# Swapped activations of block 1: shifted DMA transposes of the normalised tiles in place of copies between partition halves

## The chip, the cores and the metric

The kernel runs on one core of one Trainium2 chip. The metric is the device time of one execution in microseconds (us); the runs shown are three, with their median. Engines are named as the profile names them: PE (matrix unit, TensorE), PEld (its weight loads), DVE (VectorE), ACT (ScalarE), POOL (GpSimd), SP (SyncE, which here only issues DMAs).

## What is computed

One sequence of 2048 rows with 448 features goes through a layer norm without weights. The normalised rows feed two branches, and both are added to the input:

```python
x = A_x                                   # [1, 2048, 448] bf16
xn = _layernorm(x)
# A: 16 heads of 28, causal attention over a window of 256 keys
q, k, v = split_heads(xn @ A_wqkv)
p = softmax(where(0 <= i - j < 256, q @ k.T * 28 ** -0.5, -1e9))
a = merge_heads(p @ v) @ A_wo
# B: gated feed-forward, 448 -> 1792 -> 448
b = (gelu(xn @ B_w_gate) * (xn @ B_w_up)) @ B_w_down
return x + a + b
```

## The kernel before

**Tiling.** The 2048 rows are 16 tiles of 128 rows (`NT`), and four blocks of 512 columns once transposed (`NB`, `QB`). The 448 features are three and a half groups of 128, or seven chunks of 64. PE needs the activations with features on the partitions, so each normalised tile `xn` is transposed into `xnT`, `[128, 4, 2048]`: groups 0 to 2 hold features 0 to 383 (chunk c on the lower 64 partitions for even c, on the upper 64 for odd c), group 3 holds chunk 6, features 384 to 447, on both halves.

**Paired half matmuls.** Seven chunks of 64 rows fill half of PE's rows. The kernel therefore runs two products side by side, one on the lower half of the rows (`hi` 0), one on the upper (`hi` 1): two tiles of v (`v_pair`, L325), q and k of one group of heads (`qk_pair`, L339), two column groups of the gate or up matrix (`chunk`, L494). Each goes through all seven chunks, so each half needs every chunk on its own partitions. Chunks with `c % 2 == hi` lie there in `xnT`, chunk 6 lies on both; the others come from a copy with the halves exchanged, `xsw` `[128, 3, 1024]`. `xchunk` (L486) picks the source. `xsw` is a ring of two blocks (`ring`, L246): blocks 0 and 2 in its first 512 columns, 1 and 3 in the second.

**How the transposes and swaps are made.** Block 0's four tiles are transposed on PE (`transp`, L186). Tiles 4 to 15 are transposed by DMA from SP's queue (`dma_transp`, L182). For them `norm` (L165) writes 512 columns: the 448 features and, in columns 448 to 511, features 384 to 447 again, so that group 3 comes out with chunk 6 on both halves. `swap` (L473) then issues two DMAs from SBUF to SBUF, one for each half. Block 0 is swapped at once (L775), blocks 2 and 3 at the head of blocks 1 and 2 (L876), block 1 in two parts of two tiles each inside `ahead3`.

**Order around the change.** The order of work on each engine is written out by hand. Block 0's attention runs eight steps; the list `plan` says what is put between them. After the first steps come `ahead` (loads `wvs`, v's weights with halves exchanged), `ahead2` (statistics, `norm` and transpose of tile 4) and `ahead3` (L814): the same for tiles 5 to 7, the first part of block 1's swap, `fill_pads` on POOL, `swap_weights` (two DMAs that fill `wsq`, the exchanged weights of q and k), the second part of the swap, and the loads of `wg`, `wu`, `x_sb`, `wo` and `wd`. All those DMAs stand in SP's queue in this order, and a DMA whose input is not ready holds the queue. The first work on block 1 is `gen_pairs(1, ...)` (L847), from step 6 of block 0: v of tiles 4 and 5, v of tiles 6 and 7, then q and k of groups 0 to 2. Then block 0's gated part begins, with `wg`.

`w3p` holds the weights of q and k for chunk 6; `q_last` (L257) multiplies all 128 partitions of group 3 of `xnT` with it for heads 12 to 15, where its upper half is zero. `general_path` (L939) is a fallback behind a branch at the end, for inputs whose softmax sums leave the range; it is not taken here.

Of the kernel before, what the change touches and what calls it, by code (L numbers as in the profile page):

```python
# [16 lines left out]
S, D, H, Dh, F = 2048, 448, 16, 28, 1792  # L17
P = 128
NT = S // P
NF = F // P  # L20
QB, NB = 512, 4
# [6 lines left out]
def kernel(  # L28
# [11 lines left out]
    nc = tc.nc  # L40
# [31 lines left out]
    def rows(w, c0, n):  # L72
        return w[c0 * P:(c0 + n) * P, :].rearrange("(c p) n -> p c n", p=P)

    def load_ffn(dst, w, pairs):

        wv64 = w.rearrange("(c p) (h n) -> p c h n", p=64, h=2)
        ns = slice(pairs.start * P, pairs.stop * P)  # L80
        for hi in range(2):
            nc.sync.dma_start(out=dst[64 * hi:64 * hi + 64, :, ns], in_=wv64[:, :, hi, ns])
# [54 lines left out]
    xnT = const.tile([P, 4, S], bf16, name="xnT")  # L137
    xsw = const.tile([P, 3, 2 * QB], bf16, name="xsw")
# [24 lines left out]
    xns = {}  # L163

    def norm(t):  # L165
        xn = work.tile([P, 4, P], bf16, name="xn", bufs=4)
        xf = xn[:, :, :].rearrange("p a b -> p (a b)")
        both = ((0, D, 0), (D, 64, 384))
        for lo, n, src in both if t > 3 else both[:1]:
            nc.vector.tensor_scalar(out=xf[:, lo:lo + n], in0=x_sb[:, t, src:src + n], scalar1=mv_all[:, t, 0:1],  # L170
                                    scalar2=rstd_all[:, t:t + 1], op0=ALU.subtract, op1=ALU.mult)
        xns[t] = xn
# [8 lines left out]

    def dma_transp(t):  # L182

        nc.sync.dma_start_transpose(out=xnT[:, :, t * P:(t + 1) * P], in_=xns.pop(t)[:, :, :].rearrange("p a b -> p (a b)"))

    def transp(t, copy, tag):  # L186

# [58 lines left out]
    def ring(qb):  # L246

        return slice(qb % 2 * QB, (qb % 2 + 1) * QB)
# [39 lines left out]
    def fill_pads(last):  # L288


        def put(dst, src, n, lo):

            src = src.rearrange("p (j d) -> p j d", d=Dh)[:, :, lo:]
            if n == 4:
                nc.gpsimd.tensor_copy(out=dst[:, 12:16, Dh:32], in_=src[:, :, 24:28])
            src = src[:, :, 0:24].rearrange("p j (g i) -> p g j i", i=8)[:, :, :, 0:4]
            nc.gpsimd.tensor_copy(out=dst[:, 0:12, Dh:32].rearrange("p (g j) i -> p g j i", j=4), in_=src)

        if not last:
            for c in range(3):  # L300
                k = wraw[:, c, D + 12 * Dh:2 * D]
                put(wqp[:, c, :, :], k, 4, 0)
                put(wkp[:, c, :, :], k, 3, 4)
            return
        put(w3p[0:64, :, :], w3k[0:64, :], 4, 0)
        put(w3p[64:128, :, :], w3k[64:128, :], 3, 4)
        nc.gpsimd.memset(w3p[64:128, 12:16, :], 0.0)
# [165 lines left out]
    def swap(qb, t=None, n=4):  # L473

        t0 = P * (4 * qb if t is None else t)
        to = t0 - qb * QB + ring(qb).start
        for hi in range(2):
            nc.sync.dma_start(out=xsw[64 * hi:64 * hi + 64, :, to:to + n * P],
                              in_=xnT[64 - 64 * hi:P - 64 * hi, 0:3, t0:t0 + n * P])

    def swap_weights():

        for hi, src in enumerate((wqp, wkp)):
            nc.sync.dma_start(out=wsq[64 * hi:64 * hi + 64], in_=src[64 - 64 * hi:P - 64 * hi, 0:3])

    def xchunk(qb, hi, c, t0, n):  # L486

        r = slice(64 * hi, 64 * hi + 64)
        if c == 6 or c % 2 == hi:
            return xnT[r, c // 2, t0:t0 + n]  # L490
        t0 += ring(qb).start - qb * QB
        return xsw[r, c // 2, t0:t0 + n]

    def chunk(pair, w, p, qb, c):  # L494

# [318 lines left out]
    def ahead3():  # L814
        for t in (5, 6, 7):
            norm(t)
            dma_transp(t)
        swap(1, 4, 2)
        fill_pads(False)
        swap_weights()  # L820
        swap(1, 6, 2)
        load_ffn(wg, B_w_gate, slice(0, 3))
        load_ffn(wg, B_w_gate, slice(3, 7))
        load_ffn(wu, B_w_up, slice(5, 7))
        nc.sync.dma_start(out=x_sb[:, 12:16, :], in_=xv[:, 12:16, :])
        wo_v = A_wo.rearrange("(g j d) n -> j d g n", g=4, j=4)
        tail = A_wo[14 * Dh:, :].rearrange("(t i) n -> i t n", i=4)
        for j, (t0, n) in enumerate(SLOTS):
            nc.sync.dma_start(out=wo[32 * j:32 * j + Dh, 0:n, :], in_=wo_v[j][:, 0:n])
            nc.sync.dma_start(out=wo[32 * j + Dh:32 * j + 32, 0:n, :], in_=tail[:, t0:t0 + n])  # L830
        for k in range(0, NF, 7):
            nc.sync.dma_start(out=wd[:, k:k + 7, :], in_=rows(B_w_down, k, 7))
# [106 lines left out]
def general_path(tc, locals_):  # L939

    nc = tc.nc
    L = locals_
    x_sb, xnT, qT, kT, v_sb, wd, wo, ident = (L[k] for k in ("x_sb", "xnT", "qT", "kT", "v_sb", "wd", "wo", "ident"))
    with ExitStack() as st:
# [11 lines left out]
        swap = keep.tile([P, P], bf16, name="gswap")  # L956
        for hi in range(2):
            nc.vector.tensor_copy(out=swap[:, 64 * hi:64 * hi + 64], in_=ident[:, 64 - 64 * hi:P - 64 * hi])
        for qb in range(NB):
            ts = slice(qb * QB, (qb + 1) * QB)  # L960
            for c in range(3):
                pg = ps.tile([P, QB], f32, name="pg", tag="pg")
                nc.tensor.matmul(pg[:, :], lhsT=swap[:, :], rhs=xnT[:, c, ts], start=True, stop=True)
                nc.vector.tensor_copy(out=L["xsw"][:, c, 0:QB], in_=pg[:, :])
            for f in range(NF):
                hi, p = divmod(f, 7)
                r = slice(64 * hi, 64 * hi + 64)
                pg = ps.tile([P, QB], f32, name="pg", tag="pg")
                pu = ps.tile([P, QB], f32, name="pu", tag="pu")
                for dst, w in ((pg, L["wg"]), (pu, L["wu"])):  # L970
                    for c in range(7):
                        x = xnT[r, 3, ts] if c == 6 else xnT[r, c // 2, ts] if c % 2 == hi else L["xsw"][r, c // 2, 0:QB]
                        nc.tensor.matmul(dst[:, :], lhsT=w[r, c, p * P:(p + 1) * P], rhs=x, start=(c == 0), stop=(c == 6),
                                         tile_position=(64 * hi, 0))
                ge = wk.tile([P, QB], bf16, name="gge")
                nc.scalar.activation(out=ge[:, :], in_=pg[:, :], func=ACT.Gelu_apprx_tanh)
                nc.vector.tensor_tensor(out=hT[:, f, :], in0=ge[:, :], in1=pu[:, :], op=ALU.mult)
            for g in range(4):
                pg = ps.tile([P, QB], f32, name="pg", tag="pg")
                for c in range(4):  # L980
                    n, w = (64, L["w3p"]) if c == 3 else (P, L["wqp"][:, c, :, :])
# [3 lines left out]
            for tt in range(4):  # L985
# [6 lines left out]
                for h in range(H):  # L992
                    g, r = h // 4, slice(32 * (h % 4), 32 * (h % 4) + Dh)
# [23 lines left out]
                for j, (t0, n) in enumerate(SLOTS):  # L1017
                    c = 4 * (t0 % 7)
                    nc.vector.tensor_copy(out=o_sb[:, j:j + 4 * n - 3:4, Dh:32],
                                          in_=o_sb[:, 14 + t0 // 7, c:c + 4 * n].rearrange("p (g i) -> p g i", i=4))  # L1020
# [43 lines left out]
```

## Time and profile before

| | us |
|---|---|
| runs shown | 211.73, 211.86, 212.12; median 211.86 |
| profiled execution, its time | 212.1 |
| its span, first to last instruction | 210.3 |
| granted PE clock over the span | 1.000 |

The span is what the profile's rows are measured in, from 0 at the first instruction; the profiled execution's own time is 1.8 us longer. In the profile's groups and timelines a row names engine, source line, operation, the tile written, `<-`, the tiles read, and the shape; `x4` is a count of instructions merged into the row. Square brackets give the idle time of the engine before the row and what ended it. In SP's rows the duration is that of issuing the DMA, not of the transfer.

### The profile page before, as it was taken

The page shows a single profiled execution, that of the slowest core. Times are in us where ns is not written, and L with a number is a line of the kernel's source. Part 1 is how long each engine was busy: PE and PEld are TensorE (multiplying, and loading weights), DVE is VectorE, ACT ScalarE, POOL GpSimd, SP SyncE. Part 2 cuts the span into 40 slices and gives each one's busy share as a digit, 9 for nine tenths or more (in the row PEclk, how much of TensorE's full clock was granted, in tenths as well). Part 3 has the DMA queues.
Part 4 walks back from the last instruction along what each step waited for, and adds up shares of the span by engine and source line. Part 5 has one row for each costly group of instructions (what it writes and reads, how often), then busy time and mean ns, then how long its engine had stood idle before and what let it go on. Part 6 is the DMA issues. An engine that isn't in the chain of part 4 may idle for free. (4 is left out here: it accounts for less than half of the span.)

```text
span 210.3 us, 6672 instructions
## 1 busy us (share of the span) xinstructions
PE 205.5 (98%) x2842; PEld 98.8 (47%) x2842; DVE 156.3 (74%) x359; ACT 134.6 (64%) x132; POOL 43.8 (21%) x87
## 2 busy tenths in 40 slices
PE   7999999999999999999999999999999999999994
PEld 2444444544454445444445444544444454544572
DVE  6898899899788985696438897395385699596532
ACT  4799896956677977413778788523587787756000
POOL 5389902260000220040000112013000022032000
PEclk9999999999999999999999999999999999999999
DMA  6999989959431001003421000100000010100011
GB/s 171 254 238 230 94 199 223 248 147 254 101 88 42 25 15 28 9 4 67 75 75 47 24 4 24 23 3 20 23 5 0 3 47 3 48 5 16 3 47 50
DMA packets 24890, 15.68 MB, mean 75 GB/s; under 512 B 9208, under 2 KB 24728, under 8 KB 24856
## 3 DMA queue, kind: packets, MB, share of 16 engines
q1 hardware_dynamic: 24614, 15.04, 33.6%
q8 instruction: 23, 0.38, 0.8%
q10 hardware_dynamic: 242, 0.17, 0.3%
q14 instruction: 11, 0.09, 0.2%
HBM read 9.26 MB, written 2.41 MB: 55 GB/s over the span
## 5 line engine op out<-in xcount | busy, mean ns | idle before, releaser
L685 ACT ACTIVATE p_sb<-sc 128x2048 bf16<-128x2048 f32 x38 | 71.4, 1878 | 17.0 <-PE sc L680 12.1
L537 ACT ACTIVATE p_sb<-gt 128x1024 bf16<-128x1024 f32 x28 | 28.6, 1026 | 31.3 <-PE gt L497 30.0
L620 POOL TENSOR_TENSOR oN<-oc,l 128x512 bf16<-128x512 f32 x16 | 20.7, 1301 | 122.4 <-DVE l L633 122.4
L497 PE MATMUL gt<-xnT,wg 64*128 64x512 bf16 x224 | 45.6, 376 | 0.0
L406 PE MATMUL po<-wd,hT 128*128 128x448 bf16 (+1 forms) x224 | 44.7, 347 | 0.0
L497 PE MATMUL gt<-xsw,wg 64*128 64x512 bf16 x168 | 40.7, 376 | 0.0
L605 DVE TENSOR_TENSOR p_sb<-p_sb,masks 128x256 bf16<-128x256 bf16 (+1 forms) x98 | 30.7, 367 | 7.5 <-ACT p_sb L685 7.5
L547 DVE TENSOR_TENSOR hT<-p_sb,u 128x512 bf16<-128x512 bf16 x34 | 21.7, 675 | 13.3 <-PE u L497 13.3
L406 PEld LDWEIGHTS <-hT 128*128 128x128 bf16 x238 | 21.9, 98 | 19.1 <-issue 2.0
L497 PEld LDWEIGHTS <-wg 64*128 64x128 bf16 x392 | 19.0, 94 | 22.3
L497 PEld LDWEIGHTS <-wu 64*128 64x128 bf16 x392 | 19.1, 94 | 22.0 <-issue 0.7
L497 PE MATMUL u<-xnT,wu 64*128 64x512 bf16 x136 | 28.1, 376 | 0.0
L497 PE MATMUL u<-xsw,wu 64*128 64x512 bf16 x102 | 24.7, 376 | 0.0
L497 PE MATMUL ue<-xnT,wu 64*128 64x512 bf16 x88 | 18.1, 377 | 0.0
L639 DVE TENSOR_TENSOR oc<-oc,ov 128x512 f32<-128x512 f32 (+1 forms) x16 | 10.4, 658 | 10.1 <-ACT oc L637 9.9
L497 PE MATMUL ue<-xsw,wu 64*128 64x512 bf16 x66 | 16.2, 377 | 0.0
L680 PE MATMUL sc<-qT,kT 28*64 28x320 bf16 (+4 forms) x736 | 16.2, 259 | 0.0
L394 DVE TENSOR_TENSOR res<-po,x_sb 128x448 bf16<-128x448 f32 (+1 forms) x14 | 8.1, 605 | 7.9 <-PE po L406 6.7
L680 PEld LDWEIGHTS <-kT 28*64 28x64 bf16 x736 | 8.1, 103 | 12.2 <-issue 11.0
L514 DVE CAST hT<-ue 128x512 bf16<-128x512 f32 x16 | 10.6, 686 | 2.0 <-PE ue L497 1.9
L637 ACT COPY oc<-ov 128x512 f32<-128x512 f32 x16 | 9.3, 586 | 3.9 <-PE ov L654 3.8
L633 DVE STREAM_TRANSPOSE l<-inv_all 128x512 f32<-128x512 f32 x16 | 11.1, 700 | 0.1
(112 smaller groups left out, 278.5 us busy)
## 6 DMA issues: line engine op xcount, KB each, us to landing
out_dram<-res SPq DMA_DIRECT2D x15, 112.0 KB
wd<-in_B_w_down_dram SPq DMA_DIRECT2D x2, 784.0 KB
x_sb<-in_A_x_dram SPq DMA_DIRECT2D x3, 448.0 KB
xsw<-xnT SPq DMA_DIRECT2D x6, 192.0 KB
wu<-in_B_w_up_dram SPq DMA_DIRECT2D x4, 224.0 KB
wg<-in_B_w_gate_dram SPq DMA_DIRECT2D x2, 448.0 KB
wu<-in_B_w_up_dram SPq DMA_DIRECT2D x2, 336.0 KB
wg<-in_B_w_gate_dram SPq DMA_DIRECT2D x2, 336.0 KB
```

What stands on the lines that cost most here:

```text
L406: nc.tensor.matmul(po[:, 0:w], lhsT=x[:, k, tt * P:(tt + 1) * P], rhs=wt[:, k, lo:up], start=start and n == 0, stop=stop and n == len(term ...
L497: nc.tensor.matmul(ps, lhsT=w[64 * hi:64 * hi + 64, c, p * P:(p + 1) * P], rhs=xchunk(qb, hi, c, qb * QB, QB), start=c == 0, stop=c == 6, ...
L514: copy(out=hTs[qb][:, p + 7 * i, :], in_=us[i])
L537: nc.scalar.activation(out=ges[p][:, :, :], in_=gt[:, :, :], func=ACT.Gelu_apprx_tanh)
L547: nc.vector.tensor_tensor(out=hT[:, p + 7 * i, :], in0=ge[:, i, :], in1=u, op=ALU.mult)
L605: nc.vector.tensor_tensor(out=reg, in0=reg, in1=m, op=ALU.mult)
L620: nc.gpsimd.tensor_tensor(out=oN[:, g, :], in0=oc[:, :], in1=inv, op=ALU.mult)
L633: nc.vector.transpose(out=l1[:, :, :], in_=inv_all[:, 4 * qb + g, :].unsqueeze(2).to_broadcast([P, 16, 32]))
L637: nc.scalar.copy(out=oc[:, :], in_=ov[0][:, :])
L639: nc.vector.tensor_tensor(out=oc[:, q0:], in0=oc[:, q0:], in1=ov[1][:, q0:], op=ALU.add)
L680: nc.tensor.matmul(ss[k0:k0 + nk, j, col:col + nq], lhsT=kT[r, g, kt * P + k0:kt * P + k0 + nk], rhs=qT[r, g, ring(qb).start + q0:ring(qb) ...
L685: nc.scalar.activation(out=p_sb[:, :, 0:ncol], in_=ss[:, :, 0:ncol], func=ACT.Exp, scale=SCALE)
```

## The change

`norm` now writes features 0 to 63 into columns 448 to 511 of each tile from 4 on, in place of 384 to 447. Group 3 of `xnT` then has chunk 6 on the lower half and chunk 0 on the upper. With a view of the same tile that begins 64 columns later, features 64 to 447, a second transpose of three groups puts chunks 1, 3, 5 on the lower and 2, 4, 6 on the upper half: together with chunk 0 in `xnT` that is all that the pairs lack. For tiles 4 to 7 `dma_transp` issues this second transpose into `xsw`, and the four swap DMAs of block 1 are gone from `ahead3`. Blocks 2 and 3 keep their swap, with the upper half's copy taken from groups 1 to 3, so that the layout is the same. `xchunk` finds chunk 0 for the upper half in `xnT`, and chunks 2, 4, 6 one place lower in `xsw` than before. Block 0 is as before. `general_path` gets the same layout by one more product with its swap matrix.

v's weights (`wv`, L89) are loaded ahead of those of q and k in both kernels; the diff does not touch that.

```diff
--- before.py
+++ after.py
@@ -165,7 +165,7 @@
     def norm(t):
         xn = work.tile([P, 4, P], bf16, name="xn", bufs=4)
         xf = xn[:, :, :].rearrange("p a b -> p (a b)")
-        both = ((0, D, 0), (D, 64, 384))
+        both = ((0, D, 0), (D, 64, 0))
         for lo, n, src in both if t > 3 else both[:1]:
             nc.vector.tensor_scalar(out=xf[:, lo:lo + n], in0=x_sb[:, t, src:src + n], scalar1=mv_all[:, t, 0:1],
                                     scalar2=rstd_all[:, t:t + 1], op0=ALU.subtract, op1=ALU.mult)
@@ -181,7 +181,11 @@
 
     def dma_transp(t):
 
-        nc.sync.dma_start_transpose(out=xnT[:, :, t * P:(t + 1) * P], in_=xns.pop(t)[:, :, :].rearrange("p a b -> p (a b)"))
+        xf = xns.pop(t)[:, :, :].rearrange("p a b -> p (a b)")
+        nc.sync.dma_start_transpose(out=xnT[:, :, t * P:(t + 1) * P], in_=xf)
+        if t < 8:
+            to = ring(1).start + (t - 4) * P
+            nc.sync.dma_start_transpose(out=xsw[:, :, to:to + P], in_=xf[:, 64:D])
 
     def transp(t, copy, tag):
 
@@ -475,8 +479,9 @@
         t0 = P * (4 * qb if t is None else t)
         to = t0 - qb * QB + ring(qb).start
         for hi in range(2):
+            c0 = hi if qb else 0
             nc.sync.dma_start(out=xsw[64 * hi:64 * hi + 64, :, to:to + n * P],
-                              in_=xnT[64 - 64 * hi:P - 64 * hi, 0:3, t0:t0 + n * P])
+                              in_=xnT[64 - 64 * hi:P - 64 * hi, c0:c0 + 3, t0:t0 + n * P])
 
     def swap_weights():
 
@@ -486,10 +491,12 @@
     def xchunk(qb, hi, c, t0, n):
 
         r = slice(64 * hi, 64 * hi + 64)
+        ts = t0 + ring(qb).start - qb * QB
+        if qb and hi and c % 2 == 0:
+            return xsw[r, c // 2 - 1, ts:ts + n] if c else xnT[r, 3, t0:t0 + n]
         if c == 6 or c % 2 == hi:
             return xnT[r, c // 2, t0:t0 + n]
-        t0 += ring(qb).start - qb * QB
-        return xsw[r, c // 2, t0:t0 + n]
+        return xsw[r, c // 2, ts:ts + n]
 
     def chunk(pair, w, p, qb, c):
 
@@ -815,10 +822,8 @@
         for t in (5, 6, 7):
             norm(t)
             dma_transp(t)
-        swap(1, 4, 2)
         fill_pads(False)
         swap_weights()
-        swap(1, 6, 2)
         load_ffn(wg, B_w_gate, slice(0, 3))
         load_ffn(wg, B_w_gate, slice(3, 7))
         load_ffn(wu, B_w_up, slice(5, 7))
@@ -958,10 +963,11 @@
             nc.vector.tensor_copy(out=swap[:, 64 * hi:64 * hi + 64], in_=ident[:, 64 - 64 * hi:P - 64 * hi])
         for qb in range(NB):
             ts = slice(qb * QB, (qb + 1) * QB)
-            for c in range(3):
+            xs = [L["xsw"][:, c, 0:QB] for c in range(3)] + [L["xsw"][:, 0, QB:2 * QB]]
+            for c in range(4):
                 pg = ps.tile([P, QB], f32, name="pg", tag="pg")
                 nc.tensor.matmul(pg[:, :], lhsT=swap[:, :], rhs=xnT[:, c, ts], start=True, stop=True)
-                nc.vector.tensor_copy(out=L["xsw"][:, c, 0:QB], in_=pg[:, :])
+                nc.vector.tensor_copy(out=xs[c], in_=pg[:, :])
             for f in range(NF):
                 hi, p = divmod(f, 7)
                 r = slice(64 * hi, 64 * hi + 64)
@@ -969,7 +975,7 @@
                 pu = ps.tile([P, QB], f32, name="pu", tag="pu")
                 for dst, w in ((pg, L["wg"]), (pu, L["wu"])):
                     for c in range(7):
-                        x = xnT[r, 3, ts] if c == 6 else xnT[r, c // 2, ts] if c % 2 == hi else L["xsw"][r, c // 2, 0:QB]
+                        x = xnT[r, c // 2, ts] if c % 2 == hi else xs[c // 2][r]
                         nc.tensor.matmul(dst[:, :], lhsT=w[r, c, p * P:(p + 1) * P], rhs=x, start=(c == 0), stop=(c == 6),
                                          tile_position=(64 * hi, 0))
                 ge = wk.tile([P, QB], bf16, name="gge")
```

## The prediction

> **What bounds the kernel now.** I read the page first, then who waits for whom, then the order of time around the one wait that belongs to the edited code.
>
> ```profile
> span 210.3 us, 6672 instructions
> PE 205.5 (98%) x2842; PEld 98.8 (47%) x2842; DVE 156.3 (74%) x359; ACT 134.6 (64%) x132; POOL 43.8 (21%) x87
> ```
>
> PE is busy 98% of the span, so a transfer matters only where PE itself waits for it. The waits of PE and of its weight loads name a DMA once, and it is the swap that the change removes (columns: total us, times, longest):
>
> ```profile
> PEld L331 <- DMA xsw<-xnT: 0.5, 1, 0.5
> ```
>
> In order of time (start, duration; a row merges some instructions):
>
> ```profile
> 28.61 0.51 PE L331 MATMUL pv<-wvs,xsw 64*128 64x448 bf16 x2
> ...
> 29.37 0.51 PE L331 MATMUL pv<-wvs,xsw 64*128 64x448 bf16 x2
> 29.56 0.70 PE L331 MATMUL pv<-wv,xnT 64*128 64x448 bf16 x4
> 30.35 0.36 PE L331 MATMUL pv<-wvs,xsw 64*128 64x448 bf16 x2
> 30.55 0.35 PE L331 MATMUL pv<-wv,xnT 64*128 64x448 bf16 x2
> ...
> 30.35 0.10 PEld L331 LDWEIGHTS <-xsw 64*128 64x128 bf16 x2 [0.53 <-DMA xsw<-xnT]
> ...
> 31.50 0.10 PEld L345 LDWEIGHTS <-wsq 64*128 64x128 bf16 x2
> ...
> 36.47 0.55 PEld L497 LDWEIGHTS <-wg 64*128 64x128 bf16 x6
> ```
>
> v of tiles 4 and 5 starts at 28.6 and flows, a step every 0.19 (29.37 to 29.56, and 30.35 to 30.55). The row at 29.56 holds the last two steps of that pair (29.56 and 29.75) and the first, unswapped half-step of tiles 6 and 7. The swapped half-step that belongs with it was due at 29.94 and ran at 30.35. **PE lost 0.41 us**; the 0.53 of the row is the idle time of the loader, a little more. This is the most that taking the wait away can give there.
>
> Why the swap is late stands in SP's queue:
>
> ```profile
> 13.05 0.62 SPq L777 DMA_DIRECT2D x_sb<-in_A_x_dram  x1
> 14.47 1.26 SPq L806 DMA_DIRECT2D wvs<-in_A_wqkv_dram  x2
> 16.08 6.79 SPq L184 DMA_TRANSPOSE xnT<-xn  x4
> 24.57 1.29 SPq L478 DMA_DIRECT2D xsw<-xnT  x2
> 25.96 0.56 SPq L484 DMA_DIRECT2D wsq<-wqp  x1
> 26.62 0.54 SPq L484 DMA_DIRECT2D wsq<-wkp  x1
> 27.25 1.28 SPq L478 DMA_DIRECT2D xsw<-xnT  x2
> 28.58 3.70 SPq L82 DMA_DIRECT2D wg<-in_B_w_gate_dram  x4
> ```
>
> ```profile
> SPq L478 <- DMA xnT<-xn: 1.6, 1, 1.6
> ```
>
> The transposes of tiles 4 to 7 are issued from 16.08 to 22.87. The first swap then holds SP for 1.6 until a transpose has landed, and everything behind it waits too: both `wsq` loads, the second swap (27.25), `wg` (28.58). The second swap lands where PE goes on, at 30.35: **3.10 us after its issue began**.
>
> **The change part by part.** *norm.* The second write of each tile takes columns 0 to 63 of `x_sb` in place of 384 to 447: same shape, no cost. *Later swaps.* For blocks 2 and 3 one of the two copies takes chunks 1 to 3 in place of 0 to 2: same bytes, and those chunks come from the same transpose. *PE.* Every half-step of blocks 1 to 3 has the same shape; only its source moves between `xsw` and `xnT`. No matmul is added. *General path.* Its extra matmuls and copies lie behind a branch that this input doesn't take. These four I put at nothing; what remains is SP's queue and the transfers.
>
> *Removed:* four swap issues of 0.62 (rows below), 2.57 us of SP time, and SP's wait of 1.6. *Added:* four transposes 384 columns wide, each right behind the 512-wide one of its tile and reading the same `xn`, so none waits for a landing. The number of DMAs is unchanged, ten with the `wsq` loads, and so are the bytes: four copies of 96 KB out (row below), four transposes of 128 x 384 x 2 bytes, 96 KB, in.
>
> ```profile
> L184 SPq DMA_TRANSPOSE xnT<-xn x4: 1217/1271/2169, 16.1 to 21.7; - x4
> ...
> L478 SPq DMA_DIRECT2D xsw<-xnT x2: 616/616/617, 27.2 to 27.9; - x2
> ...
> 18.08 2.17 SPq L184 DMA_TRANSPOSE xnT<-xn  x1
> ...
> xsw<-xnT SPq DMA_DIRECT2D x4, 96.0 KB
> ...
> wsq<-wqp SPq DMA_DIRECT2D x1, 192.0 KB
> ```
>
> The issue of a 384-wide transpose isn't in this trace. Below it is bounded by the swap's 0.62, above by the 512-wide one's 1.27. With three quarters of the columns it would be 0.95 if all of the 1.27 grew with width; I take 1.1, between that and no saving. One issue of the four took 2.17, that of the second transpose, while the `x_sb` and `wvs` loads of 13.05 and 14.47 were still queued. I charge the same 0.9 extra to whichever transpose is second now, the 384-wide one of tile 4. Then the last issue ends at
>
> 16.08 + 4 x 1.27 + 4 x 1.1 + 0.9 = **26.46**.
>
> Low end: 16.08 + 4 x 1.22 + 4 x 0.62 = 23.44. High end: 16.08 + 8 x 1.27 + 0.9 = 27.14. Their inputs don't hold them up:
>
> ```profile
> 15.38 0.68 DVE L170 TENSOR_SCALAR xn<-x_sb,mv_all,rstd_all 128x448 bf16<-128x448 bf16 x2
> ...
> 17.35 2.07 DVE L170 TENSOR_SCALAR xn<-x_sb,mv_all,rstd_all 128x448 bf16<-128x448 bf16 x6
> ```
>
> DVE has tile 4 normalised at 16.06, tile 5 a third of the way into the six writes, at 18.04 (its transpose started at 18.08), and all by 19.42; with tile 4's second transpose in between, SP now comes to each later tile after it is ready.
>
> *From issue to landing* the trace gives two ends. In the busy stretch tile 5's issue ended at 20.25 and the swap that waited for it began at 24.57: 4.32. On an idle queue, late in block 1:
>
> ```profile
> 102.88 1.20 SPq L184 DMA_TRANSPOSE xnT<-xn  x1
> 105.45 0.62 SPq L478 DMA_DIRECT2D xsw<-xnT  x1
> ```
>
> the issue ended at 104.08, and the swap that waited for it began at 105.45: 1.37. So the last shifted transpose lands between 23.44 + 1.37 = 24.8 and 27.14 + 4.32 = 31.5. The input loads ahead are through by 24.6 (shown below), so I don't take the upper end but the middle, 2.85: 26.46 + 2.85 = **29.3**. PE wants the shifted tile 7 two steps after 29.94, at 30.3. The wait is gone with 1.0 us to spare.
>
> The transfers' own time doesn't set this (share of the 16 engines, GB/s, in the last two columns):
>
> ```profile
> 23.10:24.60 1.50, 1.00 2.19 171
> 24.60:26.00 1.40, 1.00 0.12 16
> 97.70:98.70 1.00, 1.00 0.66 131
> 106.50:108.60 2.10, 1.00 0.74 187
> ```
>
> The first stretch moved 256 KB, two transposes' worth, at 171 GB/s; in the second the engines stood nearly idle, so the input loads are through by then; the third has one transpose alone (128 KB within the microsecond), the fourth block 3's swap at 187. All eight transposes are 896 KB: 5.4 us at 171, 7.0 at 131, against 10.4 of issuing. [...]
>
> *What is late next.* `wsq` now goes out from 26.46, its second half by 27.6 in place of 27.16. The 96 KB swaps needed 3.10 from the first issue; `wsq` has twice their bytes, 384 against 192 KB, at 187 GB/s 1.05 us more: landing at 26.46 + 4.15 = 30.6. PE wants it at 31.50 - 0.41 = 31.09. That cover is thin, 0.5. `wg` starts about 27.7 in place of 28.58 and is used first at 36.47; PE never waited for it. What stands behind on SP comes 0.9 earlier and isn't waited for.
>
> *Does the rest follow PE?* The engine that is nearly full there is DVE:
>
> ```profile
> 30.83 0.70 DVE L633 STREAM_TRANSPOSE l<-inv_all 128x512 f32<-128x512 f32 x1
> 31.70 0.62 DVE L234 CAST v_sb<-pv 128x448 bf16<-128x448 f32 x1 [0.17 <-PE pv L331]
> 33.85 0.69 DVE L251 CAST qT<-pq 128x512 bf16<-128x512 f32 x1 [0.27 <-PE pk L345]
> 34.46 0.68 DVE L252 CAST kT<-pk 128x512 bf16<-128x512 f32 x1
> 35.20 0.37 PE L345 MATMUL pk<-xsw,wsq 64*128 64x512 bf16 x1
> ```
>
> The last row is group 2's k, which needs the PSUM bank that the copy ending at 35.14 frees: already just in time. DVE waited 0.17 + 0.27 = 0.44 for PE on the way there, so it can move up by 0.44, enough for 0.41. Behind that no wait of PE is left that could swallow the gain.
>
> *The sum:* removed stall -0.41, all else 0. The profiled execution took 212.1 (span 210.3 and 1.8 around it), so 211.7 for it; on the median of the runs shown, 211.86 - 0.41 = **211.45**.
>
> **The rivals.** *The shifted transposes come too late (slower).* Place: the swapped step of tiles 6 and 7. With the high ends above, tile 7's lands at 31.5 against 30.3: a stall of 1.2 in place of 0.41, +0.8, hence 212.65; it costs time from a landing after 30.7. `wsq`, queued behind, then lands at about 27.14 + 4.15 = 31.3, inside that stall. For it: four transposes had latencies near 4.3 in this very stretch, and now eight are in flight. Against: the loads ahead of them are through by then, and the last issue of the old four was followed by less than 4.4 (22.87 to 27.25, where SP didn't wait for it any more). [...]
>
> *The gain is used up on the way.* Either `wsq` lands after 31.09 and PE stalls there, or DVE's 0.44 isn't all usable and the k copy is late. For it: both margins are below 0.5. Between 0.1 and 0.4 is lost again: 211.55 to 211.86, say 211.7.
>
> *The transposes don't overlap.* If each waited for the one before it to land, which would undo what the edit says, eight would take 8 x (1.27 + 1.37) = 21 us: tile 7 at 37, PE 7 us late, 219. Against: the old four followed each other on SP with no wait for a landing.
>
> *More than the stall goes.* With `xsw` and `wg` early, later steps fall better in phase and another 0.2 to 0.5 comes off: 211.1. No row promises it.
>
> **How the numbers follow.** Forecast 0.48, too late 0.24, used up 0.17, more 0.08, no overlap 0.03. The likeliest gives 211.45, with its own range 211.3 to 211.6. The whole range goes from 211.0 to 212.8: below it lies half of "more", above it the worst of "too late" and the serial case. A measurement of this kernel can't tell less than about 0.2% (0.42 us) from no change, and the forecast lies on that bound: half of its chance counts as faster, half as same. Faster 0.24 + 0.08 = 0.32; same 0.24 + 0.17 = 0.41; slower 0.24 + 0.03 = 0.27.
>
> **What would show it.** In the changed trace: eight transposes on SP between 16 and 27, alternating about 1.3 and 1.1, the second one long; no wait of SP for a transpose before `wsq`; `wsq` issued near 26.5, `wg` near 27.7; PE's row of tiles 6 and 7 starting near 29.9 without a wait for `xsw`; the qk pairs 0.41 earlier and the DVE copies with them. It is wrong if a PE wait for `xsw`, `xnT` or `wsq` stands between 29.9 and 32, if a 384-wide issue takes over 1.3, or if PE's first `wg` step isn't 0.3 to 0.5 earlier while the stall is gone.

## The result, and the profile after

| | before | changed |
|---|---|---|
| median of six runs, us | 211.87 | 214.1 |
| lowest and highest, us | 211.73 and 212.12 | 213.3 and 215.51 |
| profiled execution: time, span, us | 212.1, 210.3 | 214.96, 213.2 |

The ratio of the times is 1.0114, with a 95% interval of 1.0079 to 1.0149. Ratios here and below leave out executions over 1.5% above the fastest of their kernel; of the kernel before these are 5 in 69, each with a granted clock of 0.99 over the span. The change makes the kernel slower by 2.2 us, where 0.4 less was forecast; the time lies above the predicted range.

Page of the changed kernel, the span and the busy time of each engine:

```profile
span 213.2 us, 6669 instructions
...
PE 205.8 (97%) x2837; PEld 98.7 (46%) x2842; DVE 156.2 (73%) x359; ACT 134.6 (63%) x132; POOL 43.6 (20%) x87
```

PE has the work that it had before (205.8 against 205.5), and the span is 2.9 longer: PE waits more. The view of the waits of PE in the changed kernel (total us, times, longest) says for what:

```profile
PE pk L349 <- DMA wsq<-wkp: 1.7, 1, 1.7
...
PE pk L202 <- DVE wkp L753: 0.5, 1, 0.5
```

The wait for the swap is gone. There is a wait of 1.7 for `wsq`, the exchanged weights of q and k, which the change does not touch but which stands behind the transposes in SP's queue. The second row is a wait before block 1, for a weight that is copied from an early load.

PE in order of time, changed kernel (start, duration):

```profile
29.59 0.36 PE L335 MATMUL pv<-wv,xnT 64*128 64x448 bf16 x1
...
30.92 0.35 PE L335 MATMUL pv<-wv,xnT 64*128 64x448 bf16 x1
30.95 0.35 PE L335 MATMUL pv<-wvs,xnT 64*128 64x448 bf16 x1
31.11 0.35 PE L335 MATMUL pv<-wvs,xsw 64*128 64x448 bf16 x1
...
32.25 0.38 PE L349 MATMUL pq<-xnT,wqp 64*128 64x512 bf16 x1
34.28 0.39 PE L349 MATMUL pk<-xnT,wsq 64*128 64x512 bf16 x1 [1.66 <-DMA wsq<-wkp]
...
39.28 0.38 PE L504 MATMUL gt<-xnT,wg 64*128 64x512 bf16 x1
```

Three things are to be seen. v of block 1 starts at 29.59, 1.0 later than in the profile of before (28.57). From there it flows: tiles 6 and 7 begin at 30.92 and 30.95, and the first step on a shifted transpose of theirs follows at 31.11 without a wait. Then PE starts q and k at 32.25 and stands until `wsq` has landed, at 34.28: 2.03 us from start to start, of which 1.66 are idle behind the first matmul.

SP's queue in the changed kernel:

```profile
15.98 1.26 SPq L813 DMA_DIRECT2D wvs<-in_A_wqkv_dram  x2
17.92 1.57 SPq L185 DMA_TRANSPOSE xnT<-xn  x1
19.55 1.24 SPq L188 DMA_TRANSPOSE xsw<-xn  x1
20.88 1.23 SPq L185 DMA_TRANSPOSE xnT<-xn  x1
22.16 1.25 SPq L188 DMA_TRANSPOSE xsw<-xn  x1
23.51 2.02 SPq L185 DMA_TRANSPOSE xnT<-xn  x1
25.58 1.26 SPq L188 DMA_TRANSPOSE xsw<-xn  x1
26.94 1.21 SPq L185 DMA_TRANSPOSE xnT<-xn  x1
28.20 1.26 SPq L188 DMA_TRANSPOSE xsw<-xn  x1
29.56 0.54 SPq L489 DMA_DIRECT2D wsq<-wqp  x1
30.20 0.53 SPq L489 DMA_DIRECT2D wsq<-wkp  x1
30.78 3.06 SPq L82 DMA_DIRECT2D wg<-in_B_w_gate_dram  x4
```

The eight transposes alternate as forecast, none waits for another's landing (each issue starts 0.04 to 0.10 behind the end of the one ahead), and the swaps' wait on SP is gone. But the 384-wide transpose (L188) holds SP for 1.24 to 1.26, as long as the 512-wide one (L185: 1.21 and 1.23, beside two long ones of 1.57 and 2.02). The last issue ends at 29.46, where 26.46 was forecast, and `wsq` goes out 3.1 later than forecast.

### The profile page after: what moved, and what is told of

The parts are those of the page before. It is cut to its first block, busy times and chain, and to the rows that moved or that the text cites. A ratio compares the mean times of both kernels' runs of the same rounds, so it can differ in the third digit from the quotient of the medians.

```text
span 213.2 us, 6669 instructions
## 1 busy us (share of the span) xinstructions
PE 205.8 (97%) x2837; PEld 98.7 (46%) x2842; DVE 156.2 (73%) x359; ACT 134.6 (63%) x132; POOL 43.6 (20%) x87
```

## The experiments

All ran beside the kernel before on the same chip, whose medians there were 211.84 to 211.97. The expectations name the theories themselves. Two stood at the start: that SP's longer queue makes `wsq` late, and that the changed program, as a program, starts its early work late (the 1.0 us by which v of block 1 starts behind).

**The changed kernel again, twice, and the kernel before again.** No edit.

> The changed kernel once more, unedited, for a second profile. In the first one two things were late: DVE waited 0.82 and 1.05 us for q's and k's remaining weights (L98) near 11 to 13 us, so that v of tiles 4 and 5 began at 29.59 in place of 28.57, and PE then waited 1.66 us for wsq. Theory W (wsq is late because SP issues eight transposes of 1.25 us ahead of it): the wsq wait is there again, 1.3 to 1.9 us, whatever the early part does. Theory L (the early weight load is late for a reason that belongs to this program): v of tiles 4 and 5 begins after 29.3 again. If the early lag is chance of one execution, it begins near 28.6 and the time of that execution is near 213.3.

> The kernel before again, for a second profile on this chip: v of tiles 4 and 5 at 28.6, a wait for the second swap of 0.3 to 0.5, 211.6 to 212.3. If the lag comes by chance in any program, it may stand here too, with a time above 212.5.

> The changed kernel again, a third profile: a PE wait for wsq of 1.3 to 2.0 whatever the lag, 213.3 to 215.

The changed kernel took 213.87 (213.39 to 215.08, six runs; ratio 1.0093, 1.0068 to 1.0118). Its second and third profiles show the same wait: q and k begin at 31.69 and 31.30, PE goes on with `wsq` at 34.05 and 33.32. v of block 1 starts at 29.03 and 28.64, so the late start is not in every execution, and the wait for `wsq` is.

The kernel before, profiled a second time, took 211.87. PE there:

```profile
28.75 0.36 PE L331 MATMUL pv<-wv,xnT 64*128 64x448 bf16 x1
...
29.73 0.70 PE L331 MATMUL pv<-wv,xnT 64*128 64x448 bf16 x4
30.11 0.51 PE L331 MATMUL pv<-wvs,xsw 64*128 64x448 bf16 x2
30.30 0.51 PE L331 MATMUL pv<-wv,xnT 64*128 64x448 bf16 x2
...
31.41 0.38 PE L345 MATMUL pq<-xnT,wqp 64*128 64x512 bf16 x1
...
36.43 0.38 PE L497 MATMUL gt<-xnT,wg 64*128 64x512 bf16 x1
```

The swapped step of tiles 6 and 7 (30.11) follows the one ahead of it (29.92, inside the row of 29.73) after 0.19: **the stall of 0.41 that the change was to remove is not there**, in an execution at the median of before. It belonged to the one execution that the prediction was worked from.

The third profile of the changed kernel, 215.31 us where 213.3 to 215 was expected, shows one thing more. PE in order of time, then windows (length; busy us of PE, PEld, DVE, ACT, POOL with instruction counts; granted PE clock, DMA share, GB/s):

```profile
33.32 0.39 PE L349 MATMUL pk<-xnT,wsq 64*128 64x512 bf16 x1 [1.65 <-DMA wsq<-wkp]
...
35.30 0.63 PE L349 MATMUL pq<-xnT,w3p 64*128 64x512 bf16 x1
...
35.73 0.63 PE L349 MATMUL pq<-xnT,wqp 64*128 64x512 bf16 x1
...
38.51 0.38 PE L349 MATMUL pq<-xnT,wqp 64*128 64x512 bf16 x1
...
38.72 0.38 PE L349 MATMUL pq<-xsw,wsq 64*128 64x512 bf16 x1
```

```profile
31.46:34.87 3.41, 1.76 (x35) 0.70 (x35) 2.02 (x6) 0.70 (x2) 1.26 (x1) 1.00 0.69 160
34.87:38.28 3.41, 3.41 (x18) 1.24 (x16) 2.00 (x4) 1.94 (x2) 0.00 (x0) 0.50 1.12 225
38.28:41.70 3.42, 3.42 (x40) 1.44 (x44) 2.93 (x7) 2.32 (x5) 0.00 (x0) 1.00 1.17 226
```

After the wait the granted clock falls to 0.50 for 3.41 us. The steps there come 0.43 apart (35.30 to 35.73) instead of 0.21 (38.51 to 38.72), and PE gets through 18 matmuls where the next stretch of the same length has 40. In the 3.41 us ahead of it PE was busy for 1.76 only. So this stall came with more than its own length: from v to the first gate matmul this profile takes 3.70 more than the unstalled 7.68 (table below), 2.02 for `wsq` and some 1.7 behind it. Four of the 20 profiles have such a drop between 27 and 39 us, each in or right behind a PE wait: this one, the one with the old general path (waits of 1.4 and 1.1) and the two with `wsq` on ACT (4.4 and 3.9). That the wait brings it on is read from the order of time; no run tested it by itself.

**The general path alone.** The kernel before with the changed fallback, which is not taken; and the changed kernel with the old one.

```diff
+            xs = [L["xsw"][:, c, 0:QB] for c in range(3)] + [L["xsw"][:, 0, QB:2 * QB]]
-            for c in range(3):
+            for c in range(4):
-                nc.vector.tensor_copy(out=L["xsw"][:, c, 0:QB], in_=pg[:, :])
+                nc.vector.tensor_copy(out=xs[c], in_=pg[:, :])
```

> The kernel before with only the edits of the general path, which is not taken. Theory L in the form that the larger program image makes early loads late: 212.5 to 213.0, with a wait for the weights of L98 of about 1 us in the profile. If the image does nothing: 211.9 within 0.2, and v of tiles 4 and 5 at 28.6.

> The changed kernel with the general path of the kernel before, which is not taken for this input; all else as changed. If the image makes the early lag: it is gone, and 213.3 remains (W alone, 211.9 - 0.4 + 1.8). If it does not: like the changed kernel, 213.3 to 215.5.

The first took 212.2, ratio 1.0007 (0.9995 to 1.0019): no cost. The second is as slow as the changed kernel, 1.0134 (1.01 to 1.0168). Of all profiles, that of the first has the latest start of v of block 1, 30.00, though its edit lies outside all that runs. DVE there:

```profile
12.19 0.33 DVE L746 COPY wqp<-wraw 128x336 bf16<-128x336 bf16 x1 [1.22 <-DMA wraw<-in_A_wqkv_dram]
13.36 0.32 DVE L746 COPY wkp<-wraw 128x336 bf16<-128x336 bf16 x1 [0.83 <-DMA wraw<-in_A_wqkv_dram]
```

The copies wait for the early load of the weights from HBM (the changed kernel's first profile has the same waits, 0.82 and 1.05). So the late start comes and goes from execution to execution, and the change is not needed for it. Whether the change makes it more frequent stays open: v starts at 29.0 or later in 6 of the 14 profiles with shifted transposes in the table below, and in 1 of the 4 without. The second kernel's profile has two waits, 1.4 for a shifted transpose and 1.1 for `wsq`.

**How the issue time depends on the width.** The shifted transposes take 128 columns in place of 384; the rest of block 1's swapped activations is set to zero, so this kernel leaves two thirds of that work out.

```diff
-            nc.sync.dma_start_transpose(out=xsw[:, :, to:to + P], in_=xf[:, 64:D])
+            nc.sync.dma_start_transpose(out=xsw[:, 0:1, to:to + P], in_=xf[:, 64:64 + P])
...
+    nc.gpsimd.memset(xsw[:, 1:3, QB:2 * QB], 0.0)
```

> The changed kernel with the shifted transposes cut to 128 columns, a third of their width; the other two groups of the swapped activations of block 1 are set to zero in place of being transposed, so this work is left out. If SP's issue time is that of the instruction, whatever its width: 1.2 to 1.25 us each, wsq as late as in the changed kernel, a PE wait for it of 1 to 2 us. If it grows with the columns: 0.4 to 0.7 us each, wsq issued 2.2 to 3.4 us earlier, no wait for it.

One run took 213.58. Groups of the narrow kernel by source line (ns least, median, most; first and last start), then two rows of its SP queue, a 128-wide issue and the 512-wide one behind it:

```profile
L188 SPq DMA_TRANSPOSE xsw<-xn x4: 1234/1273/2152, 17.7 to 27.6; - x4
```

```profile
24.96 1.23 SPq L188 DMA_TRANSPOSE xsw<-xn  x1
26.30 1.21 SPq L185 DMA_TRANSPOSE xnT<-xn  x1
```

**The 128-wide issue cost 1.23 to 1.31**, beside one long issue of 2.15, where the 384-wide one cost 1.24 to 1.26. With a third of the bytes in the shifted transposes `wsq` is no earlier (issued at 28.89, against 29.56, 28.77 and 28.88 in the three profiles of the changed kernel), and PE waits for it for 1.4. What delays it here is the number of transposes that SP issues, not their bytes.

**`wsq` off SP's queue.** The same two DMAs from POOL's queue, in the changed kernel (three profiles) and in the kernel before.

```diff
-            nc.sync.dma_start(out=wsq[64 * hi:64 * hi + 64], in_=src[64 - 64 * hi:P - 64 * hi, 0:3])
+            nc.gpsimd.dma_start(out=wsq[64 * hi:64 * hi + 64], in_=src[64 - 64 * hi:P - 64 * hi, 0:3])
```

> The changed kernel with the two wsq loads issued from POOL's queue, right behind the pads that they read. Theory W: the PE wait for wsq is gone; 211.4 to 212.0 if POOL's issuing (unknown here) does not hold up its masks, which PE needs at 27.7. If it does, a wait of PE for masked p_sb of 0.5 to 2 us and 212 to 213.5. Rival B: 213 or more with the wait elsewhere.

> The changed kernel with wsq on POOL's queue once more, for the profile of another execution. Whatever its time, the time above 211.76 must be found as waits. If the last shifted transposes land late by chance: a PE wait for xsw or xnT at v of tiles 6 and 7, as long as the excess. If the early weights are late: v of tiles 4 and 5 after 28.6, by as much.

> The same as the run before it, a third execution: the same two readings, told apart by where the excess over 211.76 stands.

> The kernel before with the two wsq loads issued from POOL's queue. Theory W: the second swap goes out as soon as tile 7's transpose has landed, about 26.8, and lands near 29.8, so the stall of 0.41 shrinks to 0 to 0.2: 211.4 to 211.9. It also tells whether the wide scatter of the changed kernel with this move (211.75 to 215.13) belongs to the move or to the eight transposes: scatter within 0.9 us here means the transposes, over 2 us means the move.

The changed kernel took 212.84 (211.75 to 215.13, twelve runs), 1.0045 (1.0017 to 1.0072): a good half of the loss is gone, but 211.4 to 212.0 was expected. PE in its first profile, 211.76 us, and POOL's queue:

```profile
31.17 0.38 PE L349 MATMUL pq<-xnT,wqp 64*128 64x512 bf16 x1
31.26 0.37 PE L349 MATMUL pk<-xnT,wsq 64*128 64x512 bf16 x1
...
36.25 0.38 PE L504 MATMUL gt<-xnT,wg 64*128 64x512 bf16 x1
```

```profile
23.39 0.71 POOL L489 DMA_DIRECT2D wsq<-wqp  x1
24.29 0.52 POOL L489 DMA_DIRECT2D wsq<-wkp  x1 [0.19 <-DVE st L155]
```

`wsq` is issued 6 us earlier, PE goes from v to q and k without a gap, and the first gate matmul starts at 36.25 in place of 39.28. The second profile is alike (211.90, 36.3). The third took 214.06, with another wait:

```profile
32.51 0.36 PE L335 MATMUL pv<-wvs,xsw 64*128 64x448 bf16 x2 [1.19 <-DMA xsw<-xn]
```

There tile 7's shifted transpose was late: the trace's record of landings has 15 of its 16 engines at 30.75 and the last at 32.46. The same edit on the kernel before gave 212.22 (211.77 to 213.45), 1.0018 (0.9999 to 1.0038): no gain to be told from nothing, above the 211.4 to 211.9 expected. So where `wsq` and the transposes are in time, as in the first two profiles, the changed kernel reaches the time of before (31.17 is 2.66 behind its v start of 28.51, and 31.41 in the unstalled profile of before was 2.66 behind 28.75) and does not pass it; its median stays 0.45% above, and one of its three profiles waits.

**`wsq` ahead of the last transposes.** In the changed kernel, `fill_pads` and `swap_weights` go ahead of tiles 6 and 7.

```diff
-        for t in (5, 6, 7):
-            norm(t)
-            dma_transp(t)
+        norm(5)
+        dma_transp(5)
         fill_pads(False)
         swap_weights()
+        for t in (6, 7):
+            norm(t)
+            dma_transp(t)
```

> The changed kernel with the pads and the two wsq loads moved ahead of the transposes of tiles 6 and 7. Theory W: the wsq wait of 1.66 us is gone; the last shifted transpose is issued 1.2 us later and must land by about 30.3 to 31.5, so a stall of 0 to 0.8 at v of tiles 6 and 7; 211.5 to 212.3 without the early lag, 1.0 more with it. If wsq was late for another reason than its place in SP's queue (its own transfer, the pads on POOL), the wait stays above 1 us and the time above 213.

It took 213.96, 1.0101 (1.0085 to 1.0118), where 211.5 to 212.3 was expected. SP's queue, then PE and its weight loads:

```profile
23.19 0.50 SPq L489 DMA_DIRECT2D wsq<-wqp  x1
...
29.11 2.17 SPq L188 DMA_TRANSPOSE xsw<-xn  x1
```

```profile
29.90 0.35 PE L335 MATMUL pv<-wv,xnT 64*128 64x448 bf16 x1
31.95 0.36 PE L335 MATMUL pv<-wvs,xnT 64*128 64x448 bf16 x1 [1.70 <-DMA xnT<-xn]
...
32.42 0.10 PEld L335 LDWEIGHTS <-xsw 64*128 64x128 bf16 x2 [0.36 <-DMA xsw<-xn]
```

No wait for `wsq`. Instead tile 7's transposes are last, and PE waits for both at v of tiles 6 and 7: first for the unshifted one (15 of 16 engines landed at 30.30, the last at 31.91), then for the shifted one, whose issue took 2.17, ended at 31.28 and landed at 32.38. PE's last wait in this run is for the transpose that was issued last.

**`wsq` from ACT's queue: a miss.** `nc.scalar` in place of `nc.gpsimd` above, called at the end of the fourth step of the plan, on the changed kernel and on before.

```diff
-            nc.sync.dma_start(out=wsq[64 * hi:64 * hi + 64], in_=src[64 - 64 * hi:P - 64 * hi, 0:3])
+            nc.scalar.dma_start(out=wsq[64 * hi:64 * hi + 64], in_=src[64 - 64 * hi:P - 64 * hi, 0:3])
...
-        swap_weights()
...
-            plan = [[last_v, lambda: stat(6), (u, 3), ahead], [(u, 2), ahead2, (u, 2)], [(u, 1), ahead3, (u, 7)], [(u, 8), lambda: stat(8)],
+            plan = [[last_v, lambda: stat(6), (u, 3), ahead], [(u, 2), ahead2, (u, 2)], [(u, 1), ahead3, (u, 7)], [(u, 8), lambda: stat(8), swap_weights],
```

> The changed kernel with the two wsq loads issued from ACT's queue at the end of the fourth step of block 0's attention, in place of SP's queue. Theory W (what costs the time is wsq's place behind the eight transposes): no PE wait for wsq, the last shifted transpose lands before 30.3 to 31 as in the changed kernel, no wait for it either: 211.4 to 212.0, at or below the kernel before. Rival B (the eight transposes themselves slow the DMA engines or the early part, so that any version with them is late): 213 or more, with waits elsewhere.

> The kernel before with the same move of the two wsq loads to ACT's queue. The second swap then goes out about 1.2 us earlier, at 26.0, and lands near 29.1, before PE wants it at 29.94: the stall of 0.41 goes, 211.45 to 211.6. If ACT's two issues of 0.55 us delay its softmax steps enough to reach PE: 212 to 212.6; the same addition then stands in the changed kernel with this move.

Both lose the same: 219.28, 1.0333 (1.0308 to 1.0359), and 219.13, 1.033 (1.0306 to 1.0354). ACT in the kernel before with this edit:

```profile
22.07 0.58 ACT L514 CAST hT<-ue 128x512 bf16<-128x512 f32 x1 [0.26 <-PE ue L497]
26.57 0.54 ACTq L484 DMA_DIRECT2D wsq<-wqp  x1
...
27.79 0.58 ACT L637 COPY oc<-ov 128x512 f32<-128x512 f32 x1 [5.14 <-DMA xsw<-xnT]
```

ACT has nothing to show between 22.65 and 26.57: its queue stood before the DMA, and its own copies behind it, for which PE then waited 3.9 (4.4 in the changed kernel). The semaphore records of the trace tell for what. In the profiled executions of before and of the changed kernel the DMAs of SP and ACT report their landing on eight semaphores in turn. Up to 43 us, 40 and 39 of them have another DMA ahead of them on their semaphore, and none is issued before all 16 landings of that one are on record; the first `wvs` load of the changed kernel goes out 0.02 behind the last of its sixteen (15.96 and 15.98). In the kernel before with this edit, the first `wsq` DMA shares one with tile 7's transpose, whose last engine landed at 26.49, just ahead of 26.57. In the changed kernel the two share theirs with the shifted transposes of tiles 5 and 6, landed at 26.84 and 27.95, and go out at 26.92 and 28.02. The two issued from POOL have semaphores of their own and stood for no landing: the first went out at 23.39, 0.13 behind the end of POOL's copy ahead of it, the second at 24.29 after 0.19 that DVE ended. The granted clock over the span is 0.984 to 0.992 in all executions of the two kernels. The move itself costs 7 us, so the pair tells nothing of the transposes.

**Half of the change.** Only tiles 6 and 7 get a shifted transpose; tiles 4 and 5 keep the two copies, behind the loop, of 0.6 each on SP where two transposes took 1.25 each. Three profiles; then with `wsq` from POOL; then with the copy and `wsq` ahead of tile 7.

```diff
-        if t < 8:
+        if t in (6, 7):
...
+        swap(1, 4, 2)
         fill_pads(False)
         swap_weights()
```

> The changed kernel with the shifted transposes for tiles 6 and 7 alone; tiles 4 and 5 are swapped by the two copies as in the kernel before, but issued behind all six transposes. Theory W, which counts SP's issues: six transposes end near 24.3, the copies near 25.6 without waiting, wsq near 26.8, 0.4 before its time in the kernel before; tile 7's shifted transpose lands by 28. No PE wait for xsw or wsq: 211.4 to 211.7, less than the kernel before. Rival B (any version with shifted transposes is late): 212.5 or more.

> The version with two tiles shifted again, for a second profile. If the early lag belongs to the changed programs: v of tiles 4 and 5 begins after 29.2 again, no other wait, 212.6 or more. If it is chance: it begins near 28.6 in one of two, and that execution takes 211.5 to 211.8.

> The same version, a third profile, read in the same way: v of tiles 4 and 5 after 29.2 if the lag belongs to the program, near 28.6 and 211.5 to 211.8 if it is chance.

> Two tiles shifted, and wsq issued from POOL's queue behind the pads. Theory W: wsq lands near 28, the copies of tiles 4 and 5 before 28.5, tile 7's shifted transpose near 27; no PE wait in block 1's v and qk steps, and the scatter is that of the kernel before: median 211.5 to 212.0, all runs below 213. If something else in the shifted transposes costs time: 212.5 or more, with a scatter of 2 us.

> Two tiles shifted, everything on SP, in the order transposes of tiles 5 and 6, the copies of tiles 4 and 5, wsq, the transposes of tile 7. Theory W: the copies wait up to 0.8 for tile 5's landing, wsq goes out near 25 and lands 2 us before it is used; the last transpose ends near 28 and lands near 29.5 against 30.3: the margin is now there, about 0.8, so a wait for xsw in some executions: median 211.7 to 212.4. If the order does not matter: 213.0 to 213.5 as with wsq last.

Half of the change took 213.26 (212.64 to 213.86), 1.0068 (1.0049 to 1.0087). Two of its profiles have no wait at block 1 (212.64, with v starting at 29.63, and 211.94); the third, 214.01, waits 1.4 for `wsq`:

```profile
33.57 0.39 PE L349 MATMUL pk<-xnT,wsq 64*128 64x512 bf16 x1 [1.41 <-DMA wsq<-wkp]
```

With POOL: 212.91, 1.0045 (1.0033 to 1.0058), and a wait of 0.9 for the copy. Reordered: 213.76, 1.0094 (1.008 to 1.0108), and a wait of 1.2 for tile 7's shifted transpose, issued last on SP until 29.33. No version beats the kernel before, and all three came out above what counting SP's issues gave (211.4 to 211.7, 211.5 to 212.0, 211.7 to 212.4). That any version with shifted transposes is late, the rival, is too strong: four profiles of such versions have no wait. But the count of issues leaves something out, and the landings below show it.

**All profiles in one account.** Start of v of block 1; from there to the first gate matmul, 7.68 to 7.74 in the six profiles without a wait; from there to the end of the span. In us; the last column names what PE waits for.

```
profile                      time    v start  to gate  to end  wait at block 1
before                       212.10  28.57     8.11    173.62  swap
before again                 211.87  28.75     7.68    173.67  none
before, general path alone   213.01  30.00     7.68    173.61  none
before, wsq on POOL          212.73  28.78     8.44    173.78  swap
changed                      214.96  29.59     9.70    173.92  wsq
changed again                214.38  29.03    10.02    173.64  wsq
changed, third               215.31  28.64    11.38    173.58  wsq, then clock 0.50
old general path             217.26  29.66    12.18    173.56  transpose, wsq, clock 0.50
128-wide                     213.58  28.84     9.42    173.64  wsq
wsq ahead of tiles 6, 7      213.70  28.57     9.81    173.62  transpose
changed, wsq on POOL         211.76  28.51     7.74    173.75  none
  second                     211.90  28.56     7.73    173.82  none
  third                      214.06  29.25     9.20    173.74  transpose
two tiles                    212.64  29.63     7.68    173.59  none
  second                     211.94  28.93     7.68    173.59  none
  third                      214.01  29.02     9.56    173.62  wsq
two tiles, wsq on POOL       213.23  28.93     8.80    173.77  copy
two tiles, reordered         213.47  28.89     9.25    173.56  transpose
```

The stretch from the first gate matmul to the end stays within 173.56 to 173.92 in all of them (the spans are given to 0.1, so the last column is good to 0.05): nothing that the change touches matters after 42 us. Two terms make the rest: the start of v, which varies by 1.5 between executions, and the wait.

## Why the prediction was wrong

*The step that failed is "what is late next".* It named `wsq`, put its cover at 0.5, and went on. The forecast had it landing at 30.6, wanted at 31.09. Term by term, in the three profiles of the unedited changed kernel (us; "landed" is when PE goes on):

| | forecast | changed | again | third |
|---|---|---|---|---|
| tile 4's transpose starts | 16.08 | 17.92 | 17.34 | 16.89 |
| from there to `wsq`'s issue | 10.38 | 11.64 | 11.43 | 11.99 |
| from there to landed | 4.15 | 4.72 | 5.28 | 4.44 |
| `wsq` landed | 30.6 | 34.28 | 34.05 | 33.32 |
| wanted (q and k begin) | 31.09 | 32.25 | 31.69 | 31.30 |
| PE stands | none | 2.03 | 2.36 | 2.02 |

*The issue of a 384-wide transpose, taken as 1.1.* It measured 1.25, the upper bound, and the narrow kernel shows no part of the width in it (1.23 to 1.31 at 128 columns). Four times 0.15 is 0.6. The rest of the second row's 1.1 to 1.6 is the gaps of 0.05 to 0.1 between two rows, 0.6 in all, which the forecast left out, and in the third profile longer issues: 1.86 and 2.04, where one of 2.17 was charged.

*The start of the chain, taken from one execution.* Tile 4's transpose began 0.8 to 1.8 later in the three profiles than in the first one of before. The second profile of before has it at 16.94 as well: 16.08 was an early one. What PE wanted moved less, by 0.2 to 1.2.

*From issue to landing, 4.15.* It took 0.3 to 1.1 more. The trace's record of landings shows where: `wsq`'s second half reports from 16 engines, and in the changed kernel one comes after the others. The last column is the start of a packet of 16 KB on the queue `q8 instruction` of the DMA view, by its name the one that fetches the program, the only packet of this size there between 27 and 33.2 us; the last three rows are transposes for which PE waited in other versions (us):

| | issue ends | 15th of 16 lands | last lands | packet starts |
|---|---|---|---|---|
| before | 27.16 | 29.56 | 29.56 | 30.03 |
| before again | 26.87 | 29.28 | 29.31 | 31.70 |
| changed | 30.73 | 33.09 | 34.23 | 31.11 |
| changed again | 29.95 | 32.32 | 34.00 | 30.59 |
| changed, third | 30.06 | 32.38 | 33.28 | 29.86 |
| two tiles | 29.27 | 31.62 | 31.64 | 30.95 |
| two tiles, second | 28.84 | 31.20 | 31.21 | 30.62 |
| two tiles, third | 29.35 | 31.71 | 33.52 | 30.64 |
| `wsq` ahead, tile 7's transpose | 29.06 | 30.30 | 31.91 | 29.71 |
| `wsq` on POOL, third, tile 7's shifted one | 29.65 | 30.75 | 32.46 | 30.27 |
| two tiles, reordered, tile 7's shifted one | 29.33 | 30.45 | 32.15 | 29.97 |

For `wsq`, fifteen engines take 2.3 to 2.4 throughout; the straggler adds 0.9 to 1.8. With the fifteen alone the term would have been 3.5 (33.09 less 29.56 in the first changed profile), below the 4.15. Without the straggler `wsq` would still have been late, by 0.8 (33.09 against 32.25), 0.6 and 1.1. So of PE's 2.0 to 2.4, some 0.6 to 1.1 come from the longer queue and 0.9 to 1.7 from one engine. In the third two-tile profile the fifteen had landed at 31.71, before PE came to q and k at 31.78: that wait is the straggler's alone.

In each row with a straggler the packet starts between 0.2 us before the end of the issue and 1.3 behind it; in the two rows of two tiles without one, 1.7 and 1.8 behind it. The coincidence is wider than this table. In all 20 profiles, 194 transposes, copies and `wsq` loads issued between 16 and 33 us have their 16 landings on record. A packet of 16 KB ran between the start of the issue and the 15th landing of 120 of them, and in 20 of these the last engine came 0.8 or more behind the fifteenth; of the other 74, none had a late engine. That the engine which carries the packet is the one that reports late is the author's guess from this order of time; no run here took the packet away, so the cause was not shown.

*The rival that named the place was mis-sized.* "The gain is used up on the way" had `wsq` landing after 31.09 and PE standing there, and capped the loss at 0.4, the size of the gain. Nothing in the queue capped it. And it could not cap what follows: in the third profile the clock adds some 1.7.

*The removed stall, 0.41.* The mechanism was right: SP no longer waits for a landing before the swap. But the second profile of before has no stall there, at a time of 211.87, the median. The credit was worth 0.41 in one execution and nothing in the other; set against the median, it was too much. In the two executions with `wsq` out of the way and no other wait, the changed kernel comes to the time of before, not below it.

*"The shifted transposes come too late"* is not what happened in the three profiles of the changed kernel: in the first, tile 7's lands at 30.55 and v flows. It is real all the same, and the 0.24 was not for nothing: with `wsq` on POOL or ahead of the last tiles, with two tiles reordered, or with the old general path, single executions wait 1.2 to 1.7 for a transpose. In the first three of these one engine was late, as in the table; in the last, all 16 were, 2.9 behind the end of the issue.

*The long issue, put down to the loads still queued.* Issues of 1.45 or more stand anywhere among the transposes, 40 times in 130 over all profiles. In 33 of the 40 a packet of 16 KB of the same queue was under way during the issue (in the first profile of before from 18.66 to 19.84, in the issue of 18.08 to 20.25), against 11 of the 90 shorter ones. That too is a coincidence in time.

*What held.* Norm, later swaps, PE and the general path cost nothing (the constant last stretch; 1.0007 for the general path). DVE followed PE: wherever nothing else was late, the way from v to the gate took 7.68 to 7.74. No transpose waited for another's landing (gaps of 0.04 to 0.11 between the issues in the three profiles). `wg` came late too, at 30.78 in place of 27.7, and nobody waited for it.

*What stays open:* whether the packets of 16 KB make one engine land late and an issue long, and why the early weight loads vary by up to 1.5 us, perhaps more often with the change. Of the slowest executions of the changed kernel without a profile (215.08 and 215.51, clock 1.0) it is not known which of these made them.

## What to carry to other kernels

Price an exchange of DMAs by the issue time of each instruction on its queue and by what stands behind them: here four transposes of 1.25 took the place of four copies of 0.62 plus a wait of 1.6, and the loser was a load that the edit never mentions. A margin of 0.5 us, or a stall of 0.4, read from one execution is not a term when the same rows move by 1 us between executions: profile the kernel before twice and price only what both show. If the last DMA of a full queue decides, ask which one a new order puts last: here, with `wsq` ahead, PE waited 1.70 and 0.36 for tile 7's transposes in place of 1.66 for `wsq`. The queue has to be shortened, or the load that is due sent from another engine, once it is known what its issue would wait for there: here ACT's stood for the landing of a DMA of SP (3.9 us), POOL's for none. And a queue that is timed to the last microsecond meets what the count of issues does not hold: here one engine of 16 that lands up to 1.8 late.

## What the runs showed of the hardware that was not expected

- A transpose of 128 columns held the issuing queue as long as one of 512: 1.23 to 1.31 against 1.21 to 1.33 in the narrow kernel, and two of these eight took 2.15 and 2.33 instead; over all profiles 40 of 130 transposes took 1.45 or more.
- PE's granted clock was 0.50 for 3.41 us after a wait of 2.0 (third profile of the changed kernel), and stayed at 1.00 after waits of 2.0 and 2.4 (the first two; in the first the trace has 1.00 without a change from 5.78 to 214.00). In the 3.41 us ahead of the drop PE was busy for 1.76; in the first profile it was busy for 1.75 in the 3.41 from 32.30 and the clock did not fall. What decides whether a wait is followed by such a drop was not shown.
- A DMA issued from ACT held ACT's own work for 3.9 us, until the transpose of SP's queue on whose semaphore it was to report had landed (26.49, issued at 26.57). The same DMA issued from POOL, with a semaphore of its own, cost nothing that can be measured (1.0018, 0.9999 to 1.0038).
- Of 120 DMAs during which a packet of 16 KB ran on the queue `q8 instruction`, 20 had one engine of 16 land 0.8 to 2.0 us after the others; of 74 without such a packet, none.
